# Fused attention, Mish feed-forward and routed experts on one core: zero fill and weight check pinned in the order, the logits' transposes in other banks, the last scatters untied

## The chip, the cores and the metric

One core of a Trainium2 chip runs the whole program. The metric is the device time of one execution in microseconds, as the median of several runs. Engines are named as in the profile: PE (TensorE matmul), PEld (its weight loads), DVE (VectorE), ACT (ScalarE), POOL (GpSimd), SP (SyncE, which here only issues transfers).

## What is computed

Three stages, each feeding the next:

```
state = alpha[:, :, t, :, None] * state + einsum('bhd,bhe->bhde', k[:, :, t], v[:, :, t])
y[:, :, t] = einsum('bhd,bhde->bhe', q[:, :, t], state)          # 4 x 8 heads, 768 steps, 48 wide

h = x @ w_in                                                     # x: 3072 x 384, w_in: 384 x 2048
g = h * tanh(log(1 + exp(h)))
x = g @ w_out

expert = argmax(x @ w_gate)                                      # 8 experts, one for each token
out = gate * (max(x @ w1[expert], 0) @ w2[expert])               # 384 -> 1024 -> 384
```

The gate is the softmax probability of the chosen expert.

## The kernel before

**Attention.** The 3072 tokens are cut into 24 units u0 to u23 of 128 tokens. A unit is loaded by one transfer (`load_unit`, L339; u0 in three), two scans on DVE make the running products of alpha (`a_prep1`, first scan L429, second L443), POOL scales k and q (`a_prep2`), and PE runs four small phases: transposes of k (kt), scores (qk), outputs (y) and the new state (kv). `load_unit(u + 2)` needs the buffer of unit u, so it waits for y and kv of u. Its output goes into xh and xl, a high and a low part (L532 on ACT, L533 on DVE), since every large product is made of three products of such parts.

**Feed-forward.** Three units make a tile of 384 tokens; there are 8 tiles. A tile has 16 steps f. A step is a first product of nine matmuls into a bank of `ps_h` (`mm1`, L612; the pool has three banks), a tanh on ACT (L638) and a copy on DVE (`hc`, L639) that empty the bank, two table functions for a batch of three steps (L648 to L650), a product (L655), a rounding (L656) and a difference (L658), and then a second product of nine matmuls (`mm2`, L673) that is issued six steps later into three banks that hold the tile's sum. Tile 1 comes before the second half of tile 0, so its first step is the ninth of all. The weights come as raw 64-bit words, 16 pieces (`load_w`, L346), which DVE turns into bits with three operations each (L65, L68, L71).

**Routing.** After the last step of a tile, `route` copies the three sums to SBUF (`row`, L703), transposes each into a bank (`rt`, L710), copies it back (L712), multiplies it with the gate weights (`rl`, L714), picks the expert and its slot on DVE, and scatters the three blocks of rows to a table `xs` in DRAM (L751). The SBUF tile `rt` has one buffer, and it is the one that held `zrow`, the row that the zero fill reads. The banks of `rt` and `rl` come from `ps_a`, which has two and serves the attention too.

**Zero fill.** Four transfers (`zero`, L787) fill `xs` from `zrow` before any scatter writes there.

**Weight check.** 32 loads of half a weight piece (`craw`, L824) are each looked at by two ACT operations, an absolute value (L827, a "look") and a clamp that sums up (L828).

**Experts.** The rows of each expert are loaded, transposed, and run through two products; each block of 108 results is scattered to the output by POOL (`put_out`, L938). At the end a flag that DVE made is read by all engines, which decides on a general path that is not taken here.

**What sets the order.** The program lists the early work in a table of short words (z0 to z3 are the zero fills, w the weights, m the steps). A scheduler then places the instructions of each engine by their dependences and its own estimate of time, so that what stands later in the program may run earlier; SP's transfers are placed in the same way, and each engine runs its own list strictly in turn. A dependence without a semaphore (NoSync) only fixes who stands first on an engine. When an instruction stands far ahead of its place in the table, it is the scheduler that put it there.

Of the kernel before, what the change touches and what calls it, by code (L numbers as in the profile page):

```python
# [18 lines left out]
P = 128  # L19
# [8 lines left out]
E = 8  # L28
# [248 lines left out]
def kernel(ctx: ExitStack, tc: tile.TileContext, att, w_io, w_gate, w1, w2, out):  # L277
# [52 lines left out]
        return ps_a.tile([P, 512], F32, tag="att", name=name)  # L330

    unit_t = {}

    def load_unit(u):
        if u < NU:
            unit_t[u] = work(u, "unit", (UW,), 2)
            cuts = (0, OQ, OV, UW) if u == 0 else (0, UW)
            for a, b in zip(cuts, cuts[1:]):
                nc.sync.dma_start(out=unit_t[u][:, a:b], in_=att[u][:, a:b])  # L339

    wraw = {}

    def load_w(f):
        if f < NF:
            wraw[f] = s0p.tile([P, 2 * DM], I64, tag="wraw", name="wraw", bufs=2)
            nc.sync.dma_start(out=wraw[f], in_=w_io[f])  # L346

    load_unit(0)
    load_unit(1)
# [280 lines left out]
    def act_tanh(s):  # L630
        b, i = divmod(s, KB)
        if i == 0:
            batch[b] = (
                s2p.tile([P, KB, TT], F32, tag="hc", name="hc", bufs=2),
                s2p.tile([P, KB, TT], F32, tag="tau", name="tau", bufs=2),
            )
        h, t = batch[b]
        nc.scalar.activation(out=t[:, i], in_=hbuf[s], func=AF.Tanh, scale=0.5)  # L638
        nc.vector.tensor_copy(out=h[:, i], in_=hbuf.pop(s))  # L639

    def act_mish(s):
# [36 lines left out]

    fill = []

    def after(inst, deps):
        for d in deps:
            tc.add_manual_dep(
                inst.ins, d.ins.name,
                mybir.DependencyInfo(mybir.DependencyClass.Sync, mybir.DependencyReason.DATA), reason="rows of xs"
            )

    def route(j):
# [16 lines left out]
                nc.vector.tensor_tensor(out=row[:, g, 0:DM], in0=a[g][:, 0:DM], in1=row[:, g, 0:DM], op=ALU.add)  # L705
        ls = ps_a.tile([P, 512], F32, tag="att", name="rl")[:, 0:G * E].rearrange("p (g e) -> p g e", e=E)
        for g in range(G):
            ps = ps_a.tile([P, 512], F32, tag="att", name="rt")
            for c in range(KC):
                nc.tensor.transpose(ps[:, c * P:(c + 1) * P], row[:, g, c * P:(c + 1) * P], ident)  # L710
            rt = s2p.tile([P, 1, ROW], F32, tag="rt", name="rt", bufs=1)[:, 0]
            nc.scalar.activation(out=rt[:, 0:DM], in_=ps[:, 0:DM], func=AF.Copy)  # L712
            for c in range(KC):
                nc.tensor.matmul(ls[:, g], rt[:, c * P:(c + 1) * P], wg[:, c], start=(c == 0), stop=(c == KC - 1))  # L714
# [69 lines left out]
    def zero(i):  # L784
        n = NSLOT // P
        a, b = (x * n // 4 for x in (i, i + 1))
        put = nc.sync.dma_start(  # L787
            out=xs.rearrange("(p r) d -> p r d", p=P)[:, a:b], in_=zrow.to_broadcast([P, b - a, ROW])
        )
        tc.keep_in_program_order(put)  # L790
        fill.append(put)

    def more_w(_):
# [16 lines left out]
    warm(12)  # L810
    for w in (
# [4 lines left out]
    ).split():  # L816
        does[w[0]](int(w[1:] or 0))
    s0d = ExitStack()
# [2 lines left out]
    def check_w(i):  # L821
        f, h = divmod(i, 2)
        raw = chkp[0].tile([P, DM], I64, tag="craw", name="craw", bufs=2)
        nc.sync.dma_start(out=raw, in_=w_io[f][:, h * DM:(h + 1) * DM])  # L824
        mag = chkp[0].tile([P, DM], F32, tag="mag", name="mag", bufs=1)
        hi = raw.bitcast(I32).rearrange("p (n t) -> p n t", t=2)[:, :, 1]
        nc.scalar.activation(out=mag, in_=hi.bitcast(F32), func=AF.Abs)  # L827
        nc.scalar.activation(  # L828
            out=mag, in_=mag, func=AF.Relu, scale=-1.0, bias=least, accum_out=chk_w[:, i:i + 1]
        )  # L830
# [103 lines left out]
    def put_out(e, g, ps):  # L934
        xg = ex[e][0]
        yo = s3p.tile([P, DM], F32, tag="yo", name="yo", bufs=4)
        nc.scalar.activation(out=yo[0:CG], in_=ps, func=AF.Copy, scale=xg[0:CG, g, DM:DM + 1])  # L937
        put = nc.gpsimd.indirect_dma_start(  # L938
            out=out,
            out_offset=bass.IndirectOffsetOnAxis(ap=xg[0:CG, g, DM + 1:DM + 2].bitcast(I32), axis=0),  # L940
            in_=yo[0:CG],
            in_offset=None,
            bounds_check=NT - 1,
            oob_is_err=False,
        )
        if g < CJ - 1:
            for other in outs:
                tc.declare_no_dep(put.ins, other.ins, reason="tokens have rows of their own")
            after(put, done)
            outs.append(put)  # L950
        else:
            after(put, outs)
            done[:] = [put]
            outs.clear()
# [46 lines left out]
    nst = E * NF2  # L1001
    for s in range(nst + 1):
        e, f = divmod(s, NF2)
        if s < nst:
            if f < 4:
                prep_e(e + 1, e0p if e % 2 else e1p, f)
# [11 lines left out]
    s3.close()  # L1018
    e0.close()

    redo = nc.values_load(flag[0:1, 0:1], min_val=0, max_val=3)  # L1021
    with tc.If(redo > 0):
        with tc.If(redo < 2):
            overflow(tc, xs, w1, w2, out, ident, tot)
# [61 lines left out]
```

## Time and profile before

| | |
|---|---|
| median of 3 runs | 930.66 us (926.41 to 931.54) |
| profiled execution, its own time | 930.7 us |
| its span, first to last instruction | 928.9 us |
| mean granted clock of TensorE | 0.943 |
| PE busy | 840.9 us (91%) |
| ACT busy | 549.0 us (59%) |
| DVE busy | 494.0 us (53%) |
| POOL busy | 329.4 us (35%) |

The profile's page gives busy time of each engine, and the span in 40 slices. PE is close to full in most slices, and lower in the first seven, around slices 9 to 16, and where the routed experts begin. 930.7 - 928.9 = 1.8 us lie outside the span. Since PE is the fullest engine in nearly every stretch, the views that matter are those that show where it is not full, or runs at a lower clock, and which engine or transfer it waits for there.

### The profile page before, as it was taken

Reading aid. Unit: us, or ns where it says so; the run is one execution under the profiler, and the core shown is the slowest. Engines: PE = TensorE matmul, PEld = TensorE weight load, DVE = VectorE, ACT = ScalarE, POOL = GpSimd, SP = SyncE. Lnnn points to the kernel's source line nnn. Section 1 sums busy time; section 2 is a strip of 40 time slices with the busy share of each in tenths; the row PEclk is TensorE's granted clock in tenths of the full one; section 3 lists DMA queues with packets and bytes.
Section 4 is the critical chain, followed back from the end, with each engine's and each line's share of the span. In section 5 each row is a group of like instructions: output and inputs, shape, how many; then the busy total and the mean of one; then the engine's idle time right before and its main releaser. Section 6 shows DMA issues by size and latency. Waiting matters only on the chain. (4 is left out here: it accounts for less than half of the span.)

```text
span 928.9 us, 15325 instructions
## 1 busy us (share of the span) xinstructions
PE 840.9 (91%) x6060; PEld 771.4 (83%) x6060; DVE 494.0 (53%) x907; ACT 549.0 (59%) x898; POOL 329.4 (35%) x361
## 2 busy tenths in 40 slices
PE   6777799997998997999999999898499999999994
PEld 3656589996997886899899898897399999999994
DVE  7997684545544634466464576543345543554220
ACT  2372398655777997784677586886145543554321
POOL 5877754333443424244244344133101011101111
PEclk9797599997999999899999999999599999999997
DMA  6629920112117336301202201300544534553001
GB/s 238 227 103 270 297 73 1 47 46 72 47 61 244 132 105 222 109 2 72 91 2 72 89 4 66 98 1 26 172 144 156 167 128 122 154 175 118 26 29 32
DMA packets 26620, 98.45 MB, mean 106 GB/s; under 512 B 3744, under 2 KB 9524, under 8 KB 23596
## 3 DMA queue, kind: packets, MB, share of 16 engines
q1 hardware_dynamic: 22956, 87.90, 29.4%
q0 software_dynamic: 3584, 9.50, 2.9%
q8 instruction: 49, 0.80, 0.4%
q14 instruction: 31, 0.25, 0.1%
HBM read 80.93 MB, written 17.03 MB: 105 GB/s over the span
## 5 line engine op out<-in xcount | busy, mean ns | idle before, releaser
L658 POOL TENSOR_TENSOR gl<-tau,gh 128x384 fp32r<-128x384 f32 x126 | 139.1, 1116 | 192.1 <-ACT gh L656 153.9
L655 DVE TENSOR_TENSOR tau<-tau,hc 128x384 f32<-128x384 f32 x128 | 90.7, 761 | 107.9 <-ACT tau L650 59.1
L612 PE MATMUL h<-xh,wi_h 128*128 128x384 f32 x384 | 135.3, 359 | 13.7 <-DVE hc L639 7.6
L612 PE MATMUL h<-xh,wi_l 128*128 128x384 f32 x384 | 134.4, 350 | 3.2 <-POOL wi_l L415 3.2
L612 PE MATMUL h<-xl,wi_h 128*128 128x384 f32 x384 | 135.1, 352 | 2.2 <-DVE xl L533 2.2
L673 PE MATMUL acc<-wo_h,gh 128*128 128x384 f32 x384 | 132.4, 345 | 4.6 <-ACT gh L656 4.6
L673 PE MATMUL acc<-wo_l,gh 128*128 128x384 f32 x384 | 131.4, 342 | 0.0
L673 PE MATMUL acc<-wo_h,gl 128*128 128x384 f32 x384 | 125.4, 346 | 3.7 <-POOL gl L658 3.7
L924 PE MATMUL g<-eh,ew 128*128 128x432 f32 x384 | 119.3, 365 | 0.0
L938 POOL DMA_INDIRECT out_dram<-yo,xg x32 | 31.7, 991 | 230.3 <-ACT yo L937 210.1
L969 PE MATMUL y<-hh,ew 128*128 128x432 f32 x336 | 105.1, 364 | 1.8 <-ACT hh L928 1.8
L612 PEld LDWEIGHTS h<-xh,wi_h 128*128 128x128 f32 x384 | 74.6, 196 | 19.6 <-DVE hc L639 9.3
L638 ACT ACTIVATE tau<-h 128x384 f32<-128x384 f32 x128 | 60.6, 486 | 50.2 <-PE h L612 44.2
L639 DVE COPY hc<-h 128x384 f32<-128x384 f32 x128 | 67.6, 545 | 39.1 <-ACT tau L638 39.0
L929 DVE SCALAR_TENSOR_TENSOR hl<-g,hh 128x432 fp32r<-128x432 f32 x64 | 38.5, 603 | 91.4 <-ACT hh L928 91.4
L656 ACT ACTIVATE gh<-tau 128x384 fp32r<-128x384 f32 x128 | 66.0, 522 | 35.8 <-DVE tau L655 19.9
L928 ACT ACTIVATE hh<-g 128x432 fp32r<-128x432 f32 x64 | 33.4, 524 | 82.3 <-PE g L924 81.9
L599 DVE TENSOR_TENSOR ew<-est,ew 128x512 fp32r<-128x512 f32 x96 | 61.8, 694 | 35.6 <-ACT ew L598 35.3
L673 PEld LDWEIGHTS acc<-wo_h,gh 128*128 128x128 f32 x384 | 72.9, 190 | 7.7 <-ACT gh L656 6.2
L612 PEld LDWEIGHTS h<-xh,wi_l 128*128 128x128 f32 x384 | 75.0, 195 | 4.3 <-POOL wi_l L415 3.8
L612 PEld LDWEIGHTS h<-xl,wi_h 128*128 128x128 f32 x384 | 75.2, 196 | 3.7 <-DVE xl L533 2.6
L673 PEld LDWEIGHTS acc<-wo_h,gl 128*128 128x128 f32 x384 | 71.5, 190 | 7.3 <-POOL gl L658 6.3
(150 smaller groups left out, 1665.5 us busy)
## 6 DMA issues: line engine op xcount, KB each, us to landing
unit<-in_att_dram SPq DMA_DIRECT2D x23, 1026.5 KB
est<-in_w_dram SPq DMA_DIRECT2D x28, 768.0 KB
wraw<-in_w_io_dram SPq DMA_DIRECT2D x16, 768.0 KB
craw<-in_w_io_dram SPq DMA_DIRECT2D x32, 384.0 KB
xs<-zrow SPq DMA_DIRECT2D x3, 1746.0 KB
xg<-xs SPq DMA_DIRECT2D x7, 654.8 KB
est<-in_w_dram SPq DMA_DIRECT2D x4, 512.0 KB
xs<-zrow SPq DMA_DIRECT2D x1, 1552.0 KB
```

The lines of the kernel that those rows point to most:

```text
L599: nc.vector.tensor_tensor(out=tl[:, cs], in0=tx, in1=th[:, cs].bitcast(F32), op=ALU.subtract)
L612: nc.tensor.matmul(ps, l[:, k], r[:, k], start=(n == 0), stop=(n == 3 * KC - 1))
L638: nc.scalar.activation(out=t[:, i], in_=hbuf[s], func=AF.Tanh, scale=0.5)
L639: nc.vector.tensor_copy(out=h[:, i], in_=hbuf.pop(s))
L655: nc.vector.tensor_tensor(out=t[:, x], in0=t[:, x], in1=h[:, x], op=ALU.mult)
L656: nc.scalar.activation(out=gh, in_=t[:, x], func=AF.Copy)
L658: eng.tensor_tensor(out=gl, in0=t[:, x], in1=gh.bitcast(F32), op=ALU.subtract)
L673: nc.tensor.matmul(acc[j][g][:, 0:DM], l[:, gs], w, start=first and i == 0, stop=last and i == 2)
L924: nc.tensor.matmul(ps, l[:, k, fs], r[:, k], start=(n == 0), stop=(n == 3 * KC - 1))
L928: nc.scalar.activation(out=hh, in_=ps, func=AF.Relu)
L929: nc.vector.scalar_tensor_tensor(out=hl, in0=ps, scalar=0.0, in1=hh.bitcast(F32), op0=ALU.max, op1=ALU.subtract)
L969: nc.tensor.matmul(yac[e][c], l[:, f, cs], r, start=(f == 0 and i == 0), stop=(f == NF2 - 1 and i == 2))
```

## The change

Five edits:

1. In the table, the four zero fills stand later (z0 after w14, z1 after w15, z2 after p4, z3 after p6), and each is placed on SP behind the latest load of a weight piece and of a unit.
2. Each look of the weight check is placed on ACT behind the latest tanh of the program so far.
3. The transposes `rt` take a bank of `ps_h`, the pool of the first products, instead of `ps_a`.
4. The fourth scatter of the last expert no longer waits for the three before it.
5. The flag is read in the program two experts earlier.

```
-                nc.sync.dma_start(out=unit_t[u][:, a:b], in_=att[u][:, a:b])
+                queue["u"] = nc.sync.dma_start(out=unit_t[u][:, a:b], in_=att[u][:, a:b])
...
-            nc.sync.dma_start(out=wraw[f], in_=w_io[f])
+            queue["w"] = nc.sync.dma_start(out=wraw[f], in_=w_io[f])
...
-        nc.scalar.activation(out=t[:, i], in_=hbuf[s], func=AF.Tanh, scale=0.5)
+        queue["t"] = nc.scalar.activation(out=t[:, i], in_=hbuf[s], func=AF.Tanh, scale=0.5)
...
-    def after(inst, deps):
+    def after(inst, deps, kind=mybir.DependencyClass.Sync):
...
-            ps = ps_a.tile([P, 512], F32, tag="att", name="rt")
+            ps = ps_h.tile([P, 512], F32, tag="h", name="rt")
...
         tc.keep_in_program_order(put)
+        after(put, [queue["w"], queue["u"]], mybir.DependencyClass.NoSync)
         fill.append(put)
...
-        "m3 y3 v3 a4 l5 w4 m4 b4 t4 w5 m5 q4 y4 w6 m6 v4 a5 l6 b5 w7 m7 t5 q5 y5 v5 P w8 m8 z0 a6 m9 l7 b6 w9 m10 "
-        "m11 w10 m12 z1 m13 w11 m14 m15 w12 m16 z2 m17 w13 m18 w14 m19 z3 m20 w15 S m21 p0 m22 p1 m23 p3 m24 p4 p5 "
+        "m3 y3 v3 a4 l5 w4 m4 b4 t4 w5 m5 q4 y4 w6 m6 v4 a5 l6 b5 w7 m7 t5 q5 y5 v5 P w8 m8 a6 m9 l7 b6 w9 m10 m11 "
+        "w10 m12 m13 w11 m14 m15 w12 m16 m17 w13 m18 w14 z0 m19 m20 w15 z1 S m21 p0 m22 p1 m23 p3 m24 p4 z2 p5 m25 "
...
-        nc.scalar.activation(out=mag, in_=hi.bitcast(F32), func=AF.Abs)
+        look = nc.scalar.activation(out=mag, in_=hi.bitcast(F32), func=AF.Abs)
+        after(look, [queue["t"]], mybir.DependencyClass.NoSync)
...
-        if g < CJ - 1:
+        if g < CJ - 1 or e == E - 1:
...
+        if s == nst - 2 * NF2:
+            redo = nc.values_load(flag[0:1, 0:1], min_val=0, max_val=3)
...
-    redo = nc.values_load(flag[0:1, 0:1], min_val=0, max_val=3)
     with tc.If(redo > 0):
```

**The first place is SP's list around the last weight pieces.** `wraw` is a weight piece, `unit` a unit, `xs<-zrow` a zero fill. Before, from the load of weight piece w7 on (five pieces in the first row) to the load of u7 and four more units:

```order
L346 DMA wraw<-in_w_io_dram 128x768 x5
L787 DMA xs<-zrow 128x8x388
L346 DMA wraw<-in_w_io_dram 128x768
L339 DMA unit<-in_att_dram 128x2053
L346 DMA wraw<-in_w_io_dram 128x768
L787 DMA xs<-zrow 128x9x388
L346 DMA wraw<-in_w_io_dram 128x768 x2
L787 DMA xs<-zrow 128x9x388
L339 DMA unit<-in_att_dram 128x2053
L346 DMA wraw<-in_w_io_dram 128x768
L787 DMA xs<-zrow 128x9x388
L339 DMA unit<-in_att_dram 128x2053 x5
```

With the change, from the same piece on; the lines of the code are one further down:

```order
L347 DMA wraw<-in_w_io_dram 128x768 x6
L340 DMA unit<-in_att_dram 128x2053
L347 DMA wraw<-in_w_io_dram 128x768 x4
L340 DMA unit<-in_att_dram 128x2053 x2
L787 DMA xs<-zrow 128x8x388
L787 DMA xs<-zrow 128x9x388
L340 DMA unit<-in_att_dram 128x2053
L787 DMA xs<-zrow 128x9x388 x2
L340 DMA unit<-in_att_dram 128x2053 x4
```

The first zero fill stood ahead of five weight pieces and of u5, u6 and u7. Now all weight pieces and u7 come first, two zero fills follow u7, and two follow u8.

**The same place on DVE, where the first step of tile 1 begins.** `xl` is the last input of that step, the scan `sc<-unit` with `rst_150` is the first one of a unit, and `hc` is the first copy that empties a bank. Before:

```order
L533 SCALAR_TENSOR_TENSOR xl<-y,xh 128x3x128
L429 SCALAR_TENSOR_TENSOR sc_921<-unit,rst_150 128x516
L436 TENSOR_SCALAR rc<-sc_921 128x4
L439 RECIPROCAL rc<-rc 128x4
L440 SCALAR_TENSOR_TENSOR rst_151<-sc_921,rc 128x4
L443 SCALAR_TENSOR_TENSOR sc_922<-unit,rst_151 128x516
L65 TENSOR_SCALAR wbits<-wraw 128x768
L68 SCALAR_TENSOR_TENSOR wbits<-wraw,wbits 128x768
L639 COPY hc<-h 128x384
```

With the change:

```order
L71 SCALAR_TENSOR_TENSOR wbits<-wraw,wbits 128x768
L430 SCALAR_TENSOR_TENSOR sc_920<-unit,rst_150 128x516
L437 TENSOR_SCALAR rc<-sc_920 128x4
L440 RECIPROCAL rc<-rc 128x4
L441 SCALAR_TENSOR_TENSOR rst_151<-sc_920,rc 128x4
L444 SCALAR_TENSOR_TENSOR sc_921<-unit,rst_151 128x516
L553 TENSOR_TENSOR s<-kv,sp 128x256
L745 COPY row<-ids 128x3
L748 MEMSET row 128x3x2
L534 SCALAR_TENSOR_TENSOR xl<-y,xh 128x3x128
L430 SCALAR_TENSOR_TENSOR sc_1410<-unit,rst_150 128x516
L640 COPY hc<-h 128x384
```

The scans of u6 and the last weight piece stood behind `xl`; now they stand ahead of it, and the first scan of u7 stands between `xl` and the first copy `hc`.

**The second place is SP's list where the weight check runs.** `craw` is the load of one look. Before, from the first load of a look to the last of a unit:

```order
L824 DMA craw<-in_w_io_dram 128x384 x2
L339 DMA unit<-in_att_dram 128x2053
L824 DMA craw<-in_w_io_dram 128x384 x7
L339 DMA unit<-in_att_dram 128x2053
L824 DMA craw<-in_w_io_dram 128x384 x5
L339 DMA unit<-in_att_dram 128x2053
L824 DMA craw<-in_w_io_dram 128x384 x13
L339 DMA unit<-in_att_dram 128x2053
L824 DMA craw<-in_w_io_dram 128x384 x5
L339 DMA unit<-in_att_dram 128x2053 x8
```

With the change, the first third of that stretch:

```order
L825 DMA craw<-in_w_io_dram 128x384 x2
L340 DMA unit<-in_att_dram 128x2053
L825 DMA craw<-in_w_io_dram 128x384 x3
L340 DMA unit<-in_att_dram 128x2053
L825 DMA craw<-in_w_io_dram 128x384 x4
L340 DMA unit<-in_att_dram 128x2053
L825 DMA craw<-in_w_io_dram 128x384
L340 DMA unit<-in_att_dram 128x2053
```

A unit stood behind up to 13 loads of looks; now at most five of them stand between two units, to the end. On ACT the 32 looks stood within less than two tiles; now eight stand in each of the tiles 3 to 6, each behind the tanh of an even step.

**The third place is PE's list at the end of tile 7.** `rt` are the transposes, `rl` the gate products, `rank` the counts of slots. Before:

```order
L710 MATMUL rt<-identr,row 128x128 x3
L714 MATMUL rl<-wg,rt 128x8 x3
L710 MATMUL rt<-identr,row 128x128 x3
L714 MATMUL rl<-wg,rt 128x8 x3
L710 MATMUL rt<-identr,row 128x128 x3
L714 MATMUL rl<-wg,rt 128x8 x3
```

With the change:

```order
L710 MATMUL rt<-identr,row 128x128 x9
L714 MATMUL rl<-wg,rt 128x8 x3
L726 LDWEIGHTS ones
L726 MATMUL rank<-ecap,ones 128x8
L726 LDWEIGHTS ones
L726 MATMUL rank<-cnt,ones 128x8
L714 MATMUL rl<-wg,rt 128x8 x6
```

The second and third transposes stood behind the gate product of the block before; now they stand ahead of all of them. In the tiles before that one the three transposes move up in the same way, to right behind the tile's last second product, with second products between them; the next first product, which stood ahead of the first `rt`, now stands behind the first `rl`, since the three banks of `ps_h` are taken.

The read of the flag stands where it stood on every engine: behind the last matmul on PE and behind the last scatter on POOL.

## Rows read from the trace of the kernel before

**Rows 1.** Busy time of the engines from 75 to 110 us.

```profile
core 0: us, PE busy (x) PEld busy (x) DVE busy (x) ACT busy (x) POOL busy (x), PEclk, DMA share, GB/s
75.00:110.00 35.00, 22.28 (x204) 16.54 (x202) 23.52 (x27) 10.40 (x22) 25.90 (x23) 0.60 1.02 300
```

**Rows 2.** Timeline of SP: start us, us; first zero fill, the piece behind it, u7.

```profile
71.84 0.43 SPq L787 DMA_DIRECT2D xs<-zrow  x1
76.13 0.33 SPq L346 DMA_DIRECT2D wraw<-in_w_io_dram  x1
...
109.53 1.31 SPq L339 DMA_DIRECT2D unit<-in_att_dram  x1
```

**Rows 3.** Timeline of DVE there: start us, us, [idle before <-releaser].

```profile
85.83 0.56 DVE L65 TENSOR_SCALAR wbits<-wraw 128x768 int32<-128x768 int32 x1 [4.16 <-DMA wraw<-in_w_io_dram]
...
110.01 0.56 DVE L533 SCALAR_TENSOR_TENSOR xl<-y,xh 128x384 fp32r<-128x384 f32 x1 [2.74 <-ACT xh L532]
111.90 1.23 DVE L429 TENSOR_TENSOR_SCAN sc<-unit,rst 128x516 f32<-128x516 f32 x1 [1.33 <-DMA unit<-in_att_dram]
...
118.60 0.55 DVE L639 COPY hc<-h 128x384 f32<-128x384 f32 x1
119.07 0.94 DVE L71 SCALAR_TENSOR_TENSOR wbits<-wraw,wbits 128x768 int32<-128x768 int32 x1
```

**Rows 4.** Timelines of SP and DVE: a unit's load with no other transfer, u8.

```profile
168.35 0.33 SPq L339 DMA_DIRECT2D unit<-in_att_dram  x1
...
173.31 1.23 DVE L429 TENSOR_TENSOR_SCAN sc<-unit,rst 128x516 f32<-128x516 f32 x1 [2.14 <-DMA unit<-in_att_dram]
```

**Rows 5.** Timelines of SP and ACT: two expert loads issued together, and the first one's use.

```profile
663.17 0.92 SPq L591 DMA_DIRECT2D est<-in_w_dram  x2
664.14 0.49 SPq L888 DMA_DIRECT2D xg<-xs  x1
...
671.40 1.67 ACT L598 ACTIVATE ew<-est 128x512 fp32r<-128x512 f32 x3 [3.70 <-DMA est<-in_w_dram]
```

**Rows 6.** Timeline of ACT: the first copy of a transpose.

```profile
200.03 0.49 ACT L712 ACTIVATE rt<-rt 128x384 f32<-128x384 f32 x1 [0.16 <-PE rt L710]
```

**Rows 7.** Busy time between the routings of tiles 0, 2, 3 and 4 (columns as rows 1).

```profile
261.60:343.70 82.10, 76.59 (x655) 70.80 (x654) 38.83 (x85) 70.29 (x127) 30.74 (x31) 1.00 0.45 145
343.70:415.80 72.10, 65.13 (x552) 59.14 (x551) 37.09 (x82) 58.17 (x104) 26.84 (x29) 0.93 0.36 116
415.80:487.40 71.60, 70.22 (x608) 64.59 (x607) 43.62 (x85) 46.48 (x69) 31.42 (x33) 1.00 0.15 54
```

**Rows 8.** The check's second operation (L828) in the first stretch: us, ACT busy (x).

```profile
261.60:343.70 82.10, 13.34 (x38) 1.00 0.45 145
```

**Rows 9.** Timelines of SP and DVE: looks' loads ahead of u15, and its first scan.

```profile
314.38 45.02 SPq L824 DMA_DIRECT2D craw<-in_w_io_dram  x13
359.50 0.38 SPq L339 DMA_DIRECT2D unit<-in_att_dram  x1
...
365.62 1.23 DVE L429 TENSOR_TENSOR_SCAN sc<-unit,rst 128x516 f32<-128x516 f32 x1 [4.86 <-DMA unit<-in_att_dram]
```

**Rows 10.** Timeline of ACT at the end of tile 7: second and third copies.

```profile
646.95 0.49 ACT L712 ACTIVATE rt<-rt 128x384 f32<-128x384 f32 x1 [1.37 <-PE rt L710]
648.80 0.49 ACT L712 ACTIVATE rt<-rt 128x384 f32<-128x384 f32 x1 [1.37 <-PE rt L710]
```

**Rows 11.** Timelines of ACT and POOL at the very end.

```profile
916.40 0.58 ACT L937 ACTIVATE yo<-y,xg 108x384 f32<-108x384 f32 x1 [3.03 <-issue]
...
915.31 0.99 POOL L938 DMA_INDIRECT out_dram<-yo,xg  x1 [0.30 <-issue]
919.03 0.99 POOL L938 DMA_INDIRECT out_dram<-yo,xg  x1 [2.74 <-DMA out_dram<-yo,xg]
```

**Rows 12.** Timeline of ACT: a batch of two steps, from its tanh to its roundings.

```profile
632.92 0.85 ACT L638 ACTIVATE tau<-h 128x384 f32<-128x384 f32 x2
...
639.45 0.53 ACT L656 ACTIVATE gh<-tau 128x384 fp32r<-128x384 f32 x1 [0.35 <-DVE tau L655]
```

More of the change, by code (lines that the diff above doesn't have):

```diff
@@ L332 @@
     unit_t = {}
+    queue = {}
     def load_unit(u):
@@ L679 @@
     fill = []
-    def after(inst, deps):
+    def after(inst, deps, kind=mybir.DependencyClass.Sync):
         for d in deps:
             tc.add_manual_dep(
-                inst.ins, d.ins.name,
-                mybir.DependencyInfo(mybir.DependencyClass.Sync, mybir.DependencyReason.DATA), reason="rows of xs"
+                inst.ins, d.ins.name, mybir.DependencyInfo(kind, mybir.DependencyReason.DATA), reason="in this order"
             )
```

2 rows, old and new, of the table does are left out of this document.

## The prediction, made before the change was run

> **What bounds the kernel now.** I read the page first, then busy time by stretches, then the timelines where PE is not full. PE is busy 91% of the span, and ACT, the next, 59%. So a stretch can only be shortened where PE idles or runs at a lower clock. Four such places lie where the change reaches.
>
> The first is the ramp. From 75 to 110 us PE is busy 22.3 of 35 us at a granted clock of 0.60, while the transfers are full (share 1.02, 300 GB/s) and DVE, which prepares the weights, works only 23.5 us [rows 1]. The first zero fill is issued at 71.84 and the next weight piece at 76.13 [rows 2]; DVE waits 4.2 us for that piece, until 85.83 [rows 3], 9.7 us after its issue. The larger u8, with no other transfer about, was ready 5.0 us after its issue [rows 4].
>
> The second is the weight check. In the two stretches that hold it PE idles 5.5 and 7.0 us, in the next 1.4, and in the second stretch the clock is 0.93 instead of 1.00 [rows 7]. ACT is busy 70.3 of 82.1 us in the first stretch, but 46.5 of 71.6 in the third, so it is near full where the looks are crowded. The check's second operation shows 38 records there, two for each of 19 looks [rows 8]. The loads suffer too: u15 stands behind 13 of the looks' loads and is issued at 359.50, and DVE stands 4.9 us idle for it [rows 9].
>
> The third is the routing of tile 7, which nothing covers: two copies wait 1.37 us each for their transposes [rows 10]. The fourth is the end: the last scatter starts at 919.03 after 2.74 us of waiting for the earlier scatters' data to land [rows 11].
>
> **The change part by part.** The sum is made against the profiled execution, 930.7 us, which is the median (930.66) for this purpose.
>
> *Zero fills.* Nothing is added: four transfers move. The weight pieces and u5 no longer meet them, and the scheduler then filled the time differently. Before, DVE idled 11.5 of the 35 us [rows 1]. Now the scans of u6 and the last weight piece stand ahead of xl; in the trace they ran from 111.90 to 120.01 with one copy of 0.55 between them, so 7.6 us of work move in front of it [rows 3]. If no idle time were left, xl would start at 110.0 - 11.5 + 7.6 = 106.1; if only the 4.2 us of waiting went and none of the moved work fell into the rest, at 113.4. Part of DVE's idle time is waiting for ACT, 2.7 us just before xl [rows 3], which the moved work can fill, so I take 109.
>
> Behind xl now stands the first scan of u7, and behind that the first copy hc. The load of u7 is released by the end of y of u5, at 109.53 in the trace, half a microsecond ahead of xl [rows 2, 3]. So it is issued at 108.5. Alone it needs 5.0 us [rows 4]. But two zero fills follow it at once. Where a load was issued with two others right behind it, it was ready only after 671.40 - 663.17 = 8.2 us [rows 5]. The scan takes 1.2 us, so hc comes at 108.5 + 5.0 + 1.2 = 114.7 or at 117.9, against 118.6 before. I take the middle, 116.3, a gain of 2.3, and add 0.9 for the rest of the last weight piece, which DVE did after that copy [rows 3] and now has done. **Term: 3 us gained.**
>
> The Trainium skill, "DMA: Bandwidth & Descriptors", section "Queues, rings and completion order", says that each DMA engine takes the descriptors of one issuing queue in ring order, though they need not complete in that order. By that rule the fills behind u7 would hardly delay it, the term would be 5 and the forecast 912. The 8.2 us of rows 5, where later transfers of the same queue delayed an earlier one, do not agree, so the sum keeps 3.
>
> The ends of this term: with xl at 106.1 and a lone transfer, hc comes at 111.8, a gain of about 7. With xl at 111 and an even share between the three transfers (1.05, 1.59 and 1.79 MB by their shapes, at the 300 GB/s of rows 1: 14.8 us) hc comes at 126.5, a loss of 7. The last two fills are hidden: they follow u8, issued at 168.35, and the three transfers, 4.6 MB, need 15 us at that rate, so they end near 184. The copy rt, whose buffer they read, runs at 200.03 [rows 6]. If that cover were gone, ACT would wait, and tanh behind it.
>
> *Weight check.* No look is removed, and the loads stay. What goes is the crowding. Beyond the idle time of the third stretch, the first two lose 4.1 + 5.6 = 9.7 us, and the clock costs 0.07 x 65.1 = 4.6 us; together 14.3 [rows 7]. What comes in its place: eight looks in each of four tiles. A look costs ACT (70.3 - 46.5) / 19 = 1.25 us, so eight bring a tile like the third stretch to 46.5 + 10 = 56.5 of 71.6 us, 79%, against 86% in the first [rows 7, 8]. In the first stretch PE paid 4.1 / 19 = 0.22 us a look; at that price 32 looks cost 6.9, and below the crowding they may cost nothing. I take half, 3.4. The units' loads stand behind at most five of the looks' loads, and those wait for looks that come long before the unit's own release, so no unit waits for a look. **Term: 11 gained, ends 7.4 and 14.3.**
>
> *Transposes in the first products' banks.* At the end of tile 7 all three transposes come first, and a copy then waits only for the gate product that reads the single buffer rt. I take a third of the two waits of 1.37 [rows 10]. **Term: 0.9, ends 0 and 2.7.** In the other tiles the transposes stand between second products, which cover them, and I cost them at nothing; what it costs without that cover is a rival.
>
> *Last scatter.* Its data is ready at 916.40 + 0.58 = 916.98 [rows 11]. With 0.3 us for the issue, as between the scatters before it, it starts at 917.3 instead of 919.03, and what follows it is fixed. **Term: 1.7, ends 0 and 2.7.**
>
> *Flag.* The read stands in the same place on every engine, so this edit does not do what its place in the program says. Term: 0.
>
> Sum: 3 + 11 + 0.9 + 1.7 = 16.6, and 930.7 - 16.6 = **914 us**. All low ends together give 930, all high ends 904.
>
> **The rivals.**
>
> *The zero fills collide with u7, and the looks keep their price.* For it: DVE's list has the scan of u7 ahead of the copy that PE's fourth step needs, and transfers do share [rows 5]. Against it: the shared case of rows 5 ends before the even share. With -3 for the ramp and 7.4 for the check: 930.7 - (-3 + 7.4 + 0.9 + 1.7) = 924.
>
> *The looks lengthen the batches.* Each look now stands right behind a tanh, often between it and the table functions of its batch. Some 21 batches of four tiles carry 1.5 looks each. If 0.7 us of that reached PE in each batch, the 14.3 us would be gone, and 930.7 - 5.6 = 925 would stay. Against it: second products come six steps later, and a batch of two steps took 639.98 - 632.92 = 7.1 us from tanh to rounding [rows 12], which leaves room for a look.
>
> *The first products starve in the routing (slower).* The three transposes take all three banks in which first products are made. A bank comes free when its copy is done, and the second copy waits for the first gate product. So the next first product stands behind that, and its batch starts late. If PE runs out of second products, it waits for a whole chain of 7.1 us [rows 12] in each of the six routings inside the tiles: 43 us, so 957. From 16.6 / 6 = 2.8 us a routing on, the kernel is slower than before. Against it: in PE's list of the change 45 to 54 large matmuls stand between the late batch's last first product and the second product that needs it; at the third stretch's mean of 70.22 / 608 = 0.115 us [rows 7], which counts its many small matmuls too, that is at least 5.2 us, so a routing lacks at most 1.9 us. The Trainium skill, "Perfetto Trace Analysis", section "Matmuls", asks that independent groups of matmuls rotate through different PSUM banks, so that emptying one overlaps the next; by it the borrowed banks are taken from the larger user, and this rival would be the likely one. No row of the trace before shows such a wait, since these banks held only first products.
>
> **How the numbers follow.** Forecast (the sum): 0.69. Collision with u7: 0.17. Longer batches: 0.08. Starving: 0.06. A measurement of this kernel can tell about 0.5%, 4.7 us, from no change; so faster is below 926.0. The range reaches from the high ends, 904, to the second and third case, 925, and leaves out the fourth and the tails. Faster: nearly all of the forecast (0.67), most of the second case (0.13) and half of the third (0.04), 0.84. Same: 0.10. Slower: 0.06.
>
> **What would show it.** Right: no zero fill before u7's load; DVE without waits for weight pieces; the first hc of tile 1 near 116; the looks spread over four tiles with ACT below 85% in each, and no scan waiting over 3 us for u15; copies rt at the end about 1.4 us apart; the last scatter 0.3 us behind its data. Wrong: a scan of u7 that waits longer than 8 us, ACT waiting for the gate product while first products stand still, or new idle time of PE in tiles 3 to 6 above 3 us a tile.

## The result: slower by 0.9%

| | before | changed |
|---|---|---|
| median of 6 runs, side by side | 926.84 us | 936.04 us |
| ratio, 95% interval | | 1.009 (1.006 to 1.012) |
| profiled execution: span, clock | 928.9 us, 0.943 | 936.1 us, 0.940 |
| PE busy, idle (span less busy) | 840.9, 88.0 us | 842.4, 93.7 us |

The forecast was 914 us (904 to 925), with a chance of 0.06 for slower.

The changed kernel's busy time between the same routings as [rows 7] (tiles 0 and 2, 2 and 3, 3 and 4) (columns as rows 1):

```profile
256.17:331.28 75.11, 73.08 (x629) 67.85 (x628) 39.73 (x84) 54.97 (x83) 29.19 (x30) 0.98 0.27 88
331.28:406.07 74.79, 69.57 (x582) 64.01 (x581) 40.68 (x82) 52.11 (x88) 29.20 (x30) 0.95 0.28 88
406.07:485.14 79.07, 74.86 (x633) 68.13 (x632) 44.78 (x86) 58.41 (x98) 31.24 (x33) 0.98 0.29 93
```

The first row is what the weight check's term promised: 2.0 us of PE idle instead of 5.5, ACT at 73% instead of 86%. The second still has 5.2 us of idle and a clock of 0.95. In the third, where the kernel before lost 1.4 us at a clock of 1.00, the change loses 4.2 at 0.98. The idle time has moved. Where to is told by PE's waits, the longest groups of each kernel. Before (line, releaser, us in total, times, longest):

```profile
PE t L904 <- DMA xg<-xs: 9.1, 1, 9.1
PE h L612 <- DVE hc L639: 7.6, 5, 4.4
...
PE rt L710 <- ACT row L703: 1.6, 2, 1.4
```

With the change:

```profile
PE rt L710 <- ACT row L703: 13.3, 5, 4.6
PE t L906 <- DMA xg<-xs: 9.5, 2, 9.2
...
PE rt L710 <- DVE part L705: 2.8, 1, 2.8
```

A new line stands on top: the first transposes of a tile wait for `row`, the copies of the tile's sums. The longest but one such wait is in tile 3. PE's timeline of the changed kernel there:

```profile
381.12 0.34 PE L674 MATMUL acc<-wo_h,gl 128*128 128x384 f32 x1
385.79 0.90 PE L710 MATMUL rt<-identr,row 128*128 128x128 f32 x3 [4.32 <-ACT row L703]
386.34 0.67 PE L674 MATMUL acc<-wo_h,gh 128*128 128x384 f32 x1
```

And ACT's, in the same stretch:

```profile
378.88 1.28 ACT L649 ACT_TABLE_LOAD   x1
380.18 1.26 ACT L649 ACTIVATE tau<-tau,half 128x1152 f32<-128x1152 f32 x1
381.45 1.28 ACT L650 ACT_TABLE_LOAD   x1
382.75 0.61 ACT L830 ACTIVATE mag<-mag,least 128x384 f32<-128x384 f32 x1
383.27 0.19 ACT L830 ACTIVATION_READ_ACCUMULATOR mag<-mag,least 128x1 f32 x1
383.36 1.24 ACT L651 ACTIVATE tau<-tau,quart 128x1152 f32<-128x1152 f32 x1
384.51 0.47 ACT L533 ACTIVATE xh<-y 128x384 fp32r<-128x384 f32 x1
384.88 0.47 ACT L639 ACTIVATE tau<-h 128x384 f32<-128x384 f32 x1
385.25 1.25 ACT L703 ACTIVATE row<-acc 128x384 f32<-128x384 f32 x3
```

The tile's last second product starts at 381.12. PE's next instruction is the first transpose, which needs the first row copy, and ACT is in the middle of a batch of table functions, with the second half of a look and two short operations (a rounding into `xh` and a tanh) ahead of the row copies in its list. PE stands for 4.32 us. In the kernel before two first products, 18 matmuls, stood in this place of PE's list, and the transposes found their row copies made:

```profile
393.18 0.34 PE L612 MATMUL h<-xh,wi_h 128*128 128x384 f32 x1
...
396.35 0.49 PE L710 MATMUL rt<-identr,row 128*128 128x128 f32 x3
```

With the change the matmuls behind the wait also take longer. Busy time before, in and after that stretch (PE, PEld, DVE, ACT, POOL, clock, DMA):

```profile
381.50:385.80 4.30, 0.01 (x1) 0.02 (x1) 1.17 (x3) 4.29 (x8) 0.00 (x0) 0.80 0.61 220
385.80:390.70 4.90, 4.90 (x18) 4.80 (x19) 4.69 (x8) 1.48 (x4) 3.36 (x3) 0.50 0.02 3
390.70:395.00 4.30, 4.30 (x31) 4.26 (x30) 0.95 (x1) 1.54 (x3) 3.12 (x3) 0.98 0.01 2
```

For 4.9 us behind the wait the granted clock is 0.50, the lower level of 1.2 GHz, then it is back at 2.4. In that time 18 matmuls ran; at the next row's pitch (4.30 / 31 = 0.139 us, a mix of shapes) they would have taken 2.5 us. By this estimate a wait of 4.3 us cost 4.3 + 2.4, some 6.7. Tile 6 repeats it: a wait of 4.59 us, and behind it

```profile
601.30:606.00 4.70, 4.64 (x17) 4.54 (x18) 2.60 (x5) 2.60 (x7) 1.11 (x1) 0.51 0.02 3
```

To follow the lead through the kernel I counted the large matmuls (384 columns, first and second products) in PE's timeline and compared the times at which those with the same number start, from 0 to 2303, the start of tile 7's last second product matmul. Differences to the kernel before, in us; the last three columns are runs of the next section. The profiled execution of the kernel before, 930.7 us, lies some 4 us above its median, so gains look larger here than in the medians:

| number | time before | changed | rt back | looks alone | order alone |
|---|---|---|---|---|---|
| 288 | 147.1 | +0.3 | +2.9 | -1.1 | +1.5 |
| 1080 | 345.4 | +2.5 | -2.9 | -6.8 | +2.5 |
| 1152 | 379.2 | -12.3 | -16.4 | -20.3 | -10.6 |
| 1224 | 396.6 | -4.6 | -14.6 | -18.5 | -4.0 |
| 1656 | 498.0 | +2.1 | -15.7 | -19.6 | +2.1 |
| 2232 | 629.6 | +5.7 | -11.3 | -15.3 | +9.0 |
| 2303 | 643.9 | +9.5 | -11.3 | -15.3 | +8.4 |

Between numbers 1080 and 1152 the changed kernel gains 15 us: that is the last part of the stretch in which the looks stood crowded before. It gives 8 of it back in the next 72, at tile 3's routing, and the rest and more in the routings after that.

### The profile page after: what moved, and what is told of

Read it like the earlier page. It is cut to its first block, busy times and chain, and to the rows that moved or that the text cites. A ratio compares the mean times of both kernels' runs of the same rounds, so it can differ in the third digit from the quotient of the medians.

```text
span 936.1 us, 15319 instructions
## 1 busy us (share of the span) xinstructions
PE 842.4 (90%) x6060; PEld 771.8 (82%) x6060; DVE 497.9 (53%) x907; ACT 545.8 (58%) x898; POOL 332.6 (36%) x361
## 5 line engine op out<-in xcount | busy, mean ns | idle before, releaser
L674 PE MATMUL acc<-wo_h,gh 128*128 128x384 f32 x384 | 138.4, 360 | 5.4 <-ACT gh L657 5.4
L656 DVE TENSOR_TENSOR tau<-tau,hc 128x384 f32<-128x384 f32 x128 | 83.7, 702 | 101.8 <-ACT tau L651 62.5
L613 PE MATMUL h<-xh,wi_h 128*128 128x384 f32 x384 | 133.0, 353 | 5.3 <-DVE hc L640 2.9
L613 PE MATMUL h<-xh,wi_l 128*128 128x384 f32 x384 | 132.4, 345 | 4.0 <-POOL wi_l L416 4.0
L674 PE MATMUL acc<-wo_l,gh 128*128 128x384 f32 x384 | 134.7, 351 | 0.0
L674 PEld LDWEIGHTS acc<-wo_h,gh 128*128 128x128 f32 x384 | 76.2, 198 | 9.0 <-ACT gh L657 8.0
L674 PEld LDWEIGHTS acc<-wo_h,gl 128*128 128x128 f32 x384 | 73.8, 196 | 9.9 <-POOL gl L659 8.8
```

What stands on the lines that cost most here:

```text
L613: nc.tensor.matmul(ps, l[:, k], r[:, k], start=(n == 0), stop=(n == 3 * KC - 1))
L656: nc.vector.tensor_tensor(out=t[:, x], in0=t[:, x], in1=h[:, x], op=ALU.mult)
L674: nc.tensor.matmul(acc[j][g][:, 0:DM], l[:, gs], w, start=first and i == 0, stop=last and i == 2)
```

## The experiments

Theory A: the spread looks bring what was forecast, and the place of the transposes loses more than that. B: the looks among the batches make ACT late, and that is the loss. C: the loss is the ramp. The first four runs take the change apart; the medians of the kernel before beside them are 926.96 us.

**One edit undone.**

```
-            ps = ps_h.tile([P, 512], F32, tag="h", name="rt")
+            ps = ps_a.tile([P, 512], F32, tag="att", name="rt")
```

> The change with one edit undone: the transposes take banks of ps_a again. Theory A (the loss is made in the routings: a first product can no longer run ahead of the transposes, so PE stands at the first transpose until ACT has made the row copies, and what the other edits gained is given back there): 914 to 921 us, and the 13.3 us that PE waits for row copies in the changed kernel fall below 3. Theory B (the loss comes from the looks, which now stand among the batches of four tiles and make ACT late for row copies and roundings): 930 to 936, as the looks stay where they are. Theory C (the loss comes from the ramp, where the first copy of tile 1 came later than before): 933 to 938.

Measured: 919.86 us, ratio 0.993 (0.990 to 0.995). The waits for row copies in this run, from its view of PE's waits:

```profile
PE rt L710 <- ACT row L703: 3.2, 3, 1.7
```

As theory A had it, but for 3.2 instead of under 3. The edit costs 936.04 - 919.86 = 16.2 us in the changed kernel. In the profiles the idle time of PE differs by 93.7 - (922.6 - 841.8) = 12.9 us, and the waits for `row` and `part` by 13.3 + 2.8 - 3.2 = 12.9. From number 288 to number 2232 the changed kernel falls behind this one by 5.4 + 14.2 = 19.6 us. Of these some 12 are idle time of PE (25.0 against 13.2 us), and the other 8 are longer busy time of PE for the same products (462.90 against 455.05 us), at a mean clock of 0.97 instead of 0.99. The whole span differs by less, 13.5 us, for two reasons. In the ramp, up to number 288, this profile happened to be 2.6 us later, with the same instructions in the same order there. And behind number 2232 it takes 3.6 us more: 3.7 less up to number 2303, and 7.3 more from there to the end, to which the run of the small terms comes back. B falls: the looks stayed where they are, and the loss went.

**That edit alone**, the same two lines in the kernel before, the other way round.

> The kernel before with one edit alone: the transposes take banks of ps_h. Theory A: 938 to 946 us, slower than before by 11 to 19, with over 9 us of PE waiting for row copies. Theory B: 924 to 930, no difference, since the looks stand in their old place. Theory C: 924 to 930 also.

Measured: 937.93 us, ratio 1.013 (1.010 to 1.016): slower by 11.0, with 11.4 us of waiting for row copies. One more wait of the transposes, 1.5 us, is of another kind: it ends with `hc`, the copy that empties a bank of `ps_h`. No look stands differently here. A missed its lower bound by a trifle; B and C are out.

**The looks alone.**

```
-        nc.scalar.activation(out=mag, in_=hi.bitcast(F32), func=AF.Abs)
+        look = nc.scalar.activation(out=mag, in_=hi.bitcast(F32), func=AF.Abs)
+        after(look, [queue["t"]], mybir.DependencyClass.NoSync)
```

> The kernel before with one edit alone: each look placed behind the latest tanh. Theory A: 913 to 919 us, since in the changed kernel PE had run through the first 1152 large products 12 us earlier than before, which only the spread looks can have brought. Theory B: 927 to 938, no gain or a loss. Theory C: as theory A, since the ramp is not touched.

Measured: 915.59 us, ratio 0.989 (0.986 to 0.992), so 11.4 us gained, as theories A and C had it; the term in the prediction was 11. The stretches between the same routings as the first two of [rows 7], from this run (columns as there):

```profile
258.27:331.53 73.26, 72.44 (x627) 67.52 (x625) 39.42 (x84) 55.91 (x88) 30.87 (x31) 1.00 0.30 96
331.53:403.80 72.27, 71.03 (x623) 65.54 (x622) 41.00 (x101) 56.10 (x99) 31.00 (x33) 1.00 0.32 102
```

PE idles 0.8 and 1.2 us in them, where it idled 5.5 and 7.0, and the clock stays at 1.00. (The second ends a little behind routing 3.)

**The zero fills alone**, the table's row and the NoSync dependence.

> The kernel before with one edit alone: the zero fills later in the table and behind the latest loads. Theory A: 926 to 930 us, since the 288th large product started at 147.4 us in the changed kernel against 147.1 before, so the ramp is level. Theory B: the same. Theory C: 931 to 938, slower by 4 us or more.

Measured: 928.77 us, ratio 1.001 (0.999 to 1.003): no difference. The 3 us of the sum did not come.

The next four ask why the transposes cost, and what the small terms are worth; the kernel before stands at 927.50 us beside them. A1 says it is the place in PE's list, A2 that it is the borrowed banks, the mechanism of the prediction's third rival.

**The order alone.** The transposes are in `ps_a`, as in the first run, and only their place ahead of the next first product is fixed:

```
+            if g == 0:
+                queue["r"] = trans
...
-                nc.tensor.matmul(ps, l[:, k], r[:, k], start=(n == 0), stop=(n == 3 * KC - 1))
+                mm = nc.tensor.matmul(ps, l[:, k], r[:, k], start=(n == 0), stop=(n == 3 * KC - 1))
+                if n == 0 and "r" in queue:
+                    after(mm, [queue.pop("r")], mybir.DependencyClass.NoSync)
```

> As the run with the transposes back in ps_a, but the next first product is placed on PE behind the tile's first transposes, as the changed kernel has it. Theory A1 (the place in PE's list costs: PE reaches the first transpose before ACT has made the row copy and stands there, with first products behind it that could run): 927 to 933 us, with over 8 us of PE waiting for row copies. Theory A2 (the banks cost: the next first products wait until a transposed block is copied out and multiplied, so the batch after them is late): 917 to 923, since no bank of the first products is taken here.

Measured: 941.23 us, ratio 1.014 (1.012 to 1.017). Its transposes of tile 3 in PE's timeline:

```profile
387.50 0.55 PE L712 MATMUL rt<-identr,row 128*128 128x128 f32 x3 [4.32 <-ACT row L705]
```

No bank is borrowed, and yet the same waits are there: 4.32 us in tile 3 as in the changed kernel, 2.47 against 2.66 in tile 4, 11.0 us in four waits in all. It is slower than A1 said by 8 us, and slower than the changed kernel by 5. But up to number 2303 it is level with the changed kernel (+8.4 and +9.5 in the table): the order alone, without the banks, loses as much there. The 5 us lie behind tile 7, where it takes 288.1 us to the end of the span, and the changed kernel 282.7. Against the run with the transposes back its profile has 94.0 - 80.8 = 13.2 us more idle time of PE, and at a clock of 0.937 instead of 0.940 846.4 - 841.8 = 4.6 us more busy time; A1's figure held the waits alone and not the clock behind them. What remains between 13.2 and the 10.6 us of waits for `row` and `part` that came in, and between the spans (17.8) and the medians (21.4), I did not trace.

**The banks alone.** The changed kernel with the routing cut in two behind the row copies; the rest comes two first products later in the program, its transposes still in `ps_h`:

```
+        return j, row, lg, mx, eq, oh, sm, pick, slot
+
+    def route_rest(j, row, lg, mx, eq, oh, sm, pick, slot):
...
+        if s in pend:
+            route_rest(*pend.pop(s))
...
-                return route(order[d][0])
+                r = route(order[d][0])
+                if s + 2 >= nsteps:
+                    return route_rest(*r)
+                pend[s + 2] = r
```

> The changed kernel with the routing cut in two: the row copies stay, and all that follows them comes two first products later in the program. The transposes still take all three banks of the first products, but PE has two more first products ahead of the first transpose, by which time the row copies are made. Theory A1: 916 to 924 us, with less than 3 us of waiting for row copies. Theory A2: 930 to 938, as the third first product still stands behind the first gate product.

Measured: 922.54 us, ratio 0.995 (0.993 to 0.997), as A1 said. From this run's waits of PE, and its busy time around routing 3 (PE, PEld, DVE, ACT, POOL, clock, DMA):

```profile
PE rt L713 <- ACT row L702: 0.2, 1, 0.2
```

```profile
331.00:407.00 76.00, 76.00 (x696) 70.09 (x695) 42.03 (x98) 60.26 (x100) 30.30 (x32) 1.00 0.32 97
```

The three banks are taken as before, and PE is full for 76 us on end at full clock. A2 falls, and with it the reason that the third rival gave. As a price of the banks the 922.54 - 919.86 = 2.7 us to the run with the transposes back is not clear of noise, since the intervals of the two ratios overlap, and it holds the later rest of the routing too.

**The small terms on top of the looks.** The kernel with the looks alone, with the last scatter untied and `ps_h` for the transposes of tile 7 only:

```
-        if g < CJ - 1:
+        if g < CJ - 1 or e == E - 1:
...
-            ps = ps_a.tile([P, 512], F32, tag="att", name="rt")
+            last = j == NTILE - 1
+            ps = (ps_h if last else ps_a).tile([P, 512], F32, tag="h" if last else "att", name="rt")
```

> The kernel before with the looks placed behind the latest tanh, the last scatter untied, and the transposes in ps_h in tile 7 alone, where no first product follows; zero fills and the other transposes as before. Theory A with the small terms as the changed kernel's trace gives them (0.6 us in tile 7's routing, 0.8 at the last scatter): 913 to 915.5 us, 1.4 below the run with the looks alone. If the borrowed banks cost in tile 7 too: 916 or more.

Measured: 918.64 us, ratio 0.990 (0.987 to 0.993). That lies above theory A's range, and as a time it lies where the borrowed banks would cost. But the ratios of this run and of the looks alone (0.989) can't be told apart, so the looks alone, at 915.59 us, are as good as any version here, and the two small edits are not seen in the time. The trace shows what became of them. Tile 7 in ACT's timeline of this run:

```profile
632.35 0.51 ACT L713 ACTIVATE rt<-rt 128x384 f32<-128x384 f32 x1
633.84 0.49 ACT L713 ACTIVATE rt<-rt 128x384 f32<-128x384 f32 x1 [0.98 <-PE rl L715]
...
637.69 0.22 ACT L730 ACTIVATE lg<-lg 128x24 f32<-128x24 f32 x1 [1.88 <-DVE lg L729]
```

The two waits are 0.98 us each instead of 1.37 [rows 10], the copies 1.49 apart instead of 1.85, and the routing from its first row copy to the last row shown took 637.69 - 631.22 = 6.5 us, against 651.79 - 643.94 = 7.9 before. So the borrowed banks do not cost in tile 7; they gain. But the last scatter gave almost nothing. It stands in POOL's timeline as

```profile
907.69 0.99 POOL L940 DMA_INDIRECT out_dram<-yo,xg  x1 [0.97 <-ACT yo L939]
```

It starts 0.87 us behind the start of its copy `yo`, where [rows 11] have 919.03 - 916.40 = 2.63. The span however ends 919.2 - 907.69 = 11.5 us behind that start, and in the kernel before 9.9. From the start of `yo` to the end it takes 12.4 to 12.6 us in the five profiles without this edit, and 11.7 to 12.4 in the five with it.

More than these gains is lost at the start of the experts. In PE's list of this run 24 of the transposes `t` of the experts' rows stand ahead of the first of their second products `y`, in the looks alone 20. The last four wait for DVE's `el`:

```profile
660.85 0.98 PE L906 MATMUL t<-identr,xg 108*128 108x108 f32 x4 [2.58 <-DVE el L910]
```

In the 60 us from 660 the clock is 0.94, and in the matching 60 us of the looks alone it is 1.00. From number 2303 to the end of the span this run takes 288.0 us, the kernel before 285.0, the looks alone 284.4. The runs with the transposes back, the order alone and the banks alone have 24 ahead too, waits of 2.1 to 2.6 us there, and 290.0, 288.1 and 287.5 us; the six kernels with 20 take 282.7 to 285.1. None of the edits aims at this place: it is again an order that the scheduler made, and it was not undone by itself.

**All zero fills behind u8.**

```
-        "... w14 z0 m19 m20 w15 z1 S m21 p0 m22 p1 m23 p3 m24 p4 z2 p5 m25 "
+        "... w14 m19 m20 w15 S m21 p0 m22 p1 m23 p3 m24 p4 z0 z1 z2 p5 m25 "
```

> As the run with the zero fills alone, but all four behind u8, so that none follows u7. Theory R1 (the ramp is level because the weight work that the fills had kept apart now fills DVE and POOL, which lengthen each other's operations): 926 to 930 us, as with two fills behind u7, and the first copy of tile 1 still comes after 117. Theory R2 (the two fills right behind u7 slow its load and give the gain back): 922 to 925, with the scan of u7 2 to 3 us earlier.

Measured: 934.05 us, ratio 1.008 (1.005 to 1.011): both theories missed. The load of u7, DVE's first scan of it and the copies `hc` here:

```profile
112.08 0.33 SPq L340 DMA_DIRECT2D unit<-in_att_dram  x1
```

```profile
117.25 1.23 DVE L430 TENSOR_TENSOR_SCAN sc<-unit,rst 128x516 f32<-128x516 f32 x1 [1.65 <-DMA unit<-in_att_dram]
119.14 0.56 DVE L640 COPY hc<-h 128x384 f32<-128x384 f32 x1 [0.67 <-ACT tau L639]
```

And with two fills right behind u7, in the run of the zero fills alone:

```profile
112.10 0.33 SPq L340 DMA_DIRECT2D unit<-in_att_dram  x1
112.48 1.77 SPq L787 DMA_DIRECT2D xs<-zrow  x2
```

```profile
119.20 1.23 DVE L430 TENSOR_TENSOR_SCAN sc<-unit,rst 128x516 f32<-128x516 f32 x1 [3.59 <-DMA unit<-in_att_dram]
120.36 0.53 DVE L640 COPY hc<-h 128x384 f32<-128x384 f32 x1
```

The two fills delay u7 by 1.9 us, from 5.2 behind its issue to 7.1, as R2 had it. But without them the first copy comes only 1.2 us earlier, for it then waits for the tanh of its step, and that for PE's product, and the price is paid elsewhere: four fills, 7.0 MB in all, stand ahead of the unit that is issued at 187.31, and DVE begins its scan at 202.12 instead of 191.23 with the zero fills alone. The scores' mask `am` stands behind that scan on DVE, and in PE's list the transposes of the first routing stand behind the matmuls that it frees:

```profile
207.59 0.55 PE L710 MATMUL rt<-identr,row 128*128 128x128 f32 x3 [3.76 <-DVE am L505]
```

## Why the prediction was wrong

**The step that failed** is the third of the sum: "In the other tiles the transposes stand between second products, which cover them, and I cost them at nothing." It looked at what stands behind the transposes, and not at what they need. They need the row copies, those come from ACT, and ACT runs batches of table functions, here 5.7 us long (378.88 to 383.36 + 1.24) with 0.8 of a look in it, behind which the copies stand in its list. Before, PE had two first products between the tile's last second product and the first transpose of tile 3, and they filled that time; [rows 10] are from tile 7, where no such batch is running, so they could not show it. The real term is minus 11.0 us by itself and minus 16.2 beside the other edits, instead of plus 0.9. The prediction's own sign of being wrong, new idle time above 3 us in one of the tiles 3 to 6, came in tile 3 (4.32 us) and in tile 6 (4.59).

The 16.2 is rather too small for the routings alone, because the run with the transposes back has a loss in the experts that the changed kernel does not have; from number 288 to number 2303 the two differ by 9.2 + 14.2 = 23.4 us. The same loss is near the 3 us by which that run, at 919.86, lies above the 917 that the terms measured one by one (looks 11.4, zero fills -1.8, last scatter about 0.3) would give. Why the edit costs 11.0 by itself and more beside the others stays open: each kernel has an order of its own, and the ramps of kernels with the same order there differ by up to 2.6 us at number 288.

**The third rival** had the right place and sign, and the wrong mechanism. It said that first products starve because their banks are taken; taking the banks costs 2.7 us by the medians (922.54 against 919.86, not clear of noise), and the place alone loses by number 2303 what the whole edit loses (+8.4 and +9.5). It put the price at "a whole chain of 7.1 us", 43 in all, and the point of no gain at 2.8 a routing; measured is 16.2 over the seven routings ahead of tile 7's (the prediction counted six), 2.3 each, which sufficed because the rest of the sum was smaller than forecast. What spoke against it, the 45 to 54 large matmuls ahead of the starved product, is beside the point: they stand behind the transpose that waits. The page of the Trainium skill named there, "Perfetto Trace Analysis", section "Matmuls", would have made this rival the likely one. Its sign was right, but the borrowed banks that it speaks of are the small part here.

**The weight check** was right: 11 forecast, 11.4 measured, by the mechanism given. In the changed kernel ACT is busy 73, 70 and 74% of the three stretches shown, and with the looks alone the two lesser rivals (looks that lengthen batches, looks that keep their price) did not come. Beside the moved transposes a look does reach PE: 0.8 us of the batch that PE waits for in tile 3 is one.

**The zero fills** gave nothing instead of 3 us. That the fills would let the weight work move ahead of `xl` was right: DVE worked 33.6 of the 35 us from 75 to 110, instead of 23.5 [rows 1], while the transfers' share fell from 1.02 to 0.48:

```profile
75.00:110.00 35.00, 18.35 (x170) 14.12 (x170) 33.56 (x34) 10.84 (x23) 30.30 (x25) 0.62 0.48 174
```

What failed is the path to u7: "So it is issued at 108.5". The prediction asked when DVE would be free for `xl`, and let u7 follow. But u7 is released by the end of y of u5, and y waits for the mask `am`, which POOL makes. PE before, PE with the change, and SP with the change:

```profile
107.48 1.94 PE L526 MATMUL y<-am,unit 128*32 128x128 f32 x32 [2.16 <-POOL am L499]
```

```profile
109.99 1.94 PE L527 MATMUL y<-am,unit 128*32 128x128 f32 x32 [2.18 <-POOL am L500]
```

```profile
112.02 0.33 SPq L340 DMA_DIRECT2D unit<-in_att_dram  x1
```

So u7 was issued at 112.0, 3.5 us later than forecast. It was ready 6.7 us later, close to the middle that the forecast took, and the first copy came at 119.84, 1.2 us later than before [rows 3]. `xl` came not at 109 but at 115: its `xh` is made from the same y, and ahead of `xl` a copy stood in DVE's list that waited for POOL too. DVE's timeline of the change:

```profile
113.95 1.12 DVE L745 COPY row<-ids 128x3 int32<-128x3 int32 x1 [2.62 <-POOL wo_l L416]
115.00 0.54 DVE L534 SCALAR_TENSOR_TENSOR xl<-y,xh 128x384 fp32r<-128x384 f32 x1
...
118.69 1.23 DVE L430 TENSOR_TENSOR_SCAN sc<-unit,rst 128x516 f32<-128x516 f32 x1 [3.15 <-DMA unit<-in_att_dram]
119.84 0.53 DVE L640 COPY hc<-h 128x384 f32<-128x384 f32 x1
```

POOL was late because the weight work that moved ahead is POOL's work too: in its list both masks of u5 now stand behind two weight parts (`wi_l`, `wo_l`), where one of the masks stood ahead of them before. And work takes longer there than the prediction took it, which read its 7.6 us from a stretch of 8 us in which POOL worked 3.4. DVE from 75 to 115, the kernel before (busy, mean ns):

```profile
L65 DVE TENSOR_SCALAR wbits<-wraw 128x768 int32<-128x768 int32 x5 | 4.2, 836 | 5.3 <-DMA wraw<-in_w_io_dram 5.3
L443 DVE TENSOR_TENSOR_SCAN sc<-unit,rst 128x516 f32<-128x516 f32 x2 | 2.8, 1422 | 0.1
```

The change:

```profile
L65 DVE TENSOR_SCALAR wbits<-wraw 128x768 int32<-128x768 int32 x6 | 6.9, 1144 | 0.9 <-POOL wo_l L416 0.9
L444 DVE TENSOR_TENSOR_SCAN sc<-unit,rst 128x516 f32<-128x516 f32 x2 | 3.8, 1898 | 0.1
```

With POOL busy 30.3 instead of 25.9 of the 35 us, these operations take about a third longer, and so do the first scans (1626 ns instead of 1227) and one of POOL's (`wo_l` 1598 ns instead of 1249). With the 13 operations of L68 and L71, at 142 and 127 ns more each, the 23 operations of these five groups on DVE took 5 us longer than at the durations of before. The waits for transfers that the change removed came back as longer work and as waits for POOL. That the two engines slow each other was not tried by itself. The Trainium skill, "SBUF — State Buffer", section "Who interferes with whom", says that a VectorE operation with two inputs in SBUF contends with a GpSimd operation that reads SBUF; the scans agree with it (1422 to 1898 ns). L65, which lists one input, lengthened too, and the same section names its kind, `tensor_scalar`, among those that can contend.

By the rule on ring order that the prediction took from the Trainium skill ("DMA: Bandwidth & Descriptors", section "Queues, rings and completion order"), two fills behind u7 would hardly delay it; the pair of runs with the zero fills shows 1.9 us, so the measurement decides against that reading.

**The small terms.** Tile 7's transposes gained 1.4 us in the run of the small terms and 7.9 - (660.63 - 653.41) = 0.6 in the changed one (0.9 forecast), where in exchange its last batch came later: the second products there waited 2.41 us for a rounding. The last scatter started 1.8 us earlier behind its data, as said, but "what follows it is fixed" was wrong: the end moved by 0.1 to 0.8 us.

## What to carry to other kernels

An engine that runs its list in turn pays for the operand that comes last at the *head* of what is moved: before you cost a move, ask what the first moved instruction waits for, on which engine that is made, and what stood in the gap until now. A covering row behind the instruction is no cover. And a buffer taken from another pool changes the order too: here no later user of that pool ran ahead of it any more. Keep the pool, or emit the work later, and look at the order that results, also where no edit was aimed. When a transfer is to start earlier, follow its release back to the engine that gives it, which here was POOL and not the engine that looked idle.

## What was not expected of the hardware

A wait of 4.3 us on PE is followed by 4.9 us at a granted clock of 0.50, in tile 3, and one of 4.6 by 4.7 us at 0.51 in tile 6; in tile 3 that adds about 2.4 us to the wait. DVE's and POOL's operations took 10 to 37% longer, in the means of the groups named, where both engines were nearly full, with the transfers at half of their former share. And an earlier start of the last scatter, by 1.8 us, moved the end by less than 1 us.
